# Reordering a Fourier mixing kernel: the last inverse stage later behind its reads, the first transforms sooner, a table in portions, and a bias added from PSUM

## The chip, the cores and the metric

The kernel runs on one core of a Trainium2 chip. The time is device microseconds from start to end of one execution; the span in a profile is some 1.8 us shorter. Each kernel was run several times beside the kernel before on the same chip. A ratio below is the mean time of one kernel's fast runs over that of the other's fast runs of the same rounds, so it is not quite the ratio of the medians quoted beside it.

## The reference

Two layers follow each other on `x` of 8 batches, 3072 positions and 256 channels. Cut to what matters:

```python
X = np.fft.rfft(x, axis=1)                       # along the sequence
Yr = Xr @ w_r - Xi @ w_i + b_r                   # complex product with bias
Yi = Xr @ w_i + Xi @ w_r + b_i
Y  = sign(Y) * maximum(abs(Y) - 0.01, 0)         # soft threshold, each part
y  = np.fft.irfft(Y, n=3072, axis=1)
xk, xr = mixes of y with y shifted by one position
k  = maximum(xk @ w_k, 0)
out = sigmoid(xr @ w_r) * (k * k @ w_v)
```

The transform of length 3072 is split into 96 x 32. So each batch goes through four stages of matmuls ("first", "second" with the mix, "back", "last"), and between first and second, and between back and last, the data goes through DRAM to be turned: A is stored and read back, then V is stored and read back. The "tokens" are the second layer, 6 blocks of 512 positions per batch.

## The kernel before

The program order of every engine is fixed while the kernel is built. A small list scheduler keeps a clock in microseconds and estimates when each buffer will be ready, and emits the unit with the smallest due time among those that its clock holds ready. If the estimate was too early, TensorE stands at that unit, and what is ordered after it waits too (5.5 us for V in the profiled run below). The parts that the change touches:

```python
READ_US, WRITE_US = 7.0, 5.0            # the scheduler's estimates

# first stage: evict, store A, read it back turned
def store(k):
    nc.sync.dma_start(out=Adr[b][:, 8 * q:8 * q + 8, :], in_=a)
    ...                                  # also starts a later batch's load of x
    if q == 3:
        at(k + WRITE_US, fetch)          # fetch: 8 reads of A, 192 KB each, same queue

# mix: z = PSUM; z += bias; y = soft threshold of z
e = copy(k, z, ps, 1.03, 1.22)           # on ScalarE or VectorE
nc.vector.tensor_tensor(out=z, in0=z, in1=bias, op=ALU.add)
nc.vector.tensor_scalar(out=y, in0=z, scalar1=LAM, scalar2=-LAM, op0=ALU.min, op1=ALU.max)
nc.vector.tensor_tensor(out=y, in0=z, in1=y, op=ALU.subtract)

# back: evict V, store it, read it back turned
for q in (2, 3, 0, 1):
    nc.sync.dma_start(out=V2[b, q], in_=Vdr[b][:, 8 * q:8 * q + 8, :])
done["V2", b] = k + READ_US              # when the last stage may be ordered
...
fb += first(b, s - 0.9 * P, s - 0.2 * P) # due times; P = 71.5 us is one batch's period
fa += middle(b, s, s + 0.5 * P)          # second, mix, back
fc += last(b, s + 0.75 * P, s + 0.95 * P)
```

V stores, V reads, A stores, A reads and output stores all leave through one queue, that of SyncE; loads of x leave through GpSimd's.

## Time and profile before

| | before |
|---|---|
| median of whole runs (range), us | 607.5 (602.77 to 610.39), 4 runs; the prediction knew three of them, median 608.08 |
| span of the profiled run, us | 604.4 |
| TensorE busy | 570.7 us, 94% |
| TensorE waits for V from DRAM | 5.5 us |
| time at half clock, without the end | 6.8 us in two stretches |
| start of the last stage, batch to batch | 71.4 us (mean of batches 2 to 6) |

"Busy" is time with an instruction in flight. A group's line ends with the engine's idle time ahead of it and what ended that idle time, as `<-`. "PE" is TensorE, "PEld" its weight loads, "DVE" VectorE, "ACT" ScalarE, and "SPq" the instructions of SyncE that issue DMA. The prediction below shows the lines of before.

### The profile page before, as it was taken

Reading aid. Unit: us, or ns where it says so; the run is one execution under the profiler, and the core shown is the slowest. Engines: PE = TensorE matmul, PEld = TensorE weight load, DVE = VectorE, ACT = ScalarE, POOL = GpSimd, SP = SyncE. Lnnn points to the kernel's source line nnn. Section 1 sums busy time; section 2 is a strip of 40 time slices with the busy share of each in tenths; the row PEclk is TensorE's granted clock in tenths of the full one; section 3 lists DMA queues with packets and bytes.
Section 4 is the critical chain, followed back from the end, with each engine's and each line's share of the span. In section 5 each row is a group of like instructions: output and inputs, shape, how many; then the busy total and the mean of one; then the engine's idle time right before and its main releaser. Section 6 shows DMA issues by size and latency. Waiting matters only on the chain.

```text
span 604.4 us, 12322 instructions
## 1 busy us (share of the span) xinstructions
PE 570.7 (94%) x4823; PEld 430.9 (71%) x4891; DVE 517.6 (86%) x839; ACT 436.3 (72%) x477; POOL 23.9 (4%) x53
## 2 busy tenths in 40 slices
PE   4977999999999999889999999999999999999996
PEld 3856766677767787667776777677776778776775
DVE  7677998789998899958988888979988889989983
ACT  6956986767776777567786768777787777667553
POOL 7001000000000000000000000000000000000000
PEclk9999999999999999989999999999999999999999
DMA  8945849864589555793569935785347834362224
GB/s 149 158 87 129 171 96 240 190 129 106 107 202 213 142 123 119 173 222 99 124 133 225 203 77 117 159 247 125 94 104 186 185 96 89 80 183 50 65 64 102
DMA packets 68878, 84.06 MB, mean 139 GB/s; under 512 B 9042, under 2 KB 53844, under 8 KB 68820
## 3 DMA queue, kind: packets, MB, share of 16 engines
q1 hardware_dynamic: 62916, 68.98, 45.8%
q0 software_dynamic: 5712, 14.03, 14.9%
q8 instruction: 38, 0.62, 0.4%
q10 hardware_dynamic: 192, 0.26, 0.2%
q14 instruction: 20, 0.16, 0.1%
HBM read 50.07 MB, written 47.19 MB: 161 GB/s over the span
## 4 chain that ended last, share of the span: by engine, by line
PE 80%; DMA 7%; DVE 5%; ACT 5%; issue 2%; SPq 1%; POOL 0%; ACTq 0%; POOLq 0%; DVEq 0%
PE banks L655 25%; PE banks L611 24%; PE banks L422 12%; PE banks L638 6%; DMA V<-Vdr 4%; PE banks L448 3%; PE banks L394 3%; PE banks L279 3%; PE banks L525 3%; ACT rl L617 2%; DMA Vdr<-V 2%; DMA xs<-in_x_dram 1%; ACT YT L226 1%; PE banks L352 1%; DVE Y L438 1%
## 5 line engine op out<-in xcount | busy, mean ns | idle before, releaser
L617 ACT ACTIVATE rl<-banks 128x1024 bf16<-128x1024 f32 x192 | 195.5, 1033 | 76.2 <-PE banks L611 75.2
L611 PE MATMUL banks<-xk,wk 128*128 128x512 bf16 x700 | 190.6, 379 | 5.3 <-ACT A L226 0.8
L655 PE MATMUL banks<-wv,k 128*128 128x256 bf16 x1536 | 183.4, 272 | 0.3 <-DVE k L623 0.3
L655 PEld LDWEIGHTS <-k 128*128 128x128 bf16 x1536 | 149.7, 98 | 30.3 <-issue 1.2
L623 DVE TENSOR_TENSOR k<-rl 128x1024 bf16<-128x1024 bf16 x192 | 131.1, 686 | 17.9 <-ACT rl L617 17.2
L611 PEld LDWEIGHTS <-wk 128*128 128x128 bf16 x768 | 73.0, 98 | 59.7 <-issue 3.5
L422 PEld LDWEIGHTS <-XT 128*128 128x128 bf16 x768 | 74.1, 98 | 17.2 <-issue 1.2
L422 PE MATMUL banks<-wr,XT 128*128 128x256 bf16 x384 | 73.3, 272 | 0.5 <-ACT YT L226 0.2
L422 PE MATMUL banks<-wi,XT 128*128 128x256 bf16 x384 | 73.3, 273 | 0.4 <-DVE XT L404 0.4
L589 DVE SCALAR_TENSOR_TENSOR xk<-diff,muk,YT 128x512 bf16<-128x512 bf16 x96 | 70.0, 745 | 0.5
L589 DVE SCALAR_TENSOR_TENSOR xr<-diff,mur,YT 128x512 bf16<-128x512 bf16 x96 | 68.9, 745 | 0.0
L666 DVE TENSOR_TENSOR o<-banks,rg 128x1024 f32<-128x1024 f32 (+1 forms) x49 | 58.7, 1197 | 5.8 <-PE banks L655 5.8
L226 ACT ACTIVATE YT<-banks 128x768 bf16<-128x768 f32 x60 | 46.4, 815 | 21.7 <-PE banks L525 19.0
L226 ACT ACTIVATE XT<-banks 128x1024 bf16<-128x1024 f32 (+2 forms) x46 | 44.9, 982 | 14.5 <-PE banks L394 14.3
L226 ACT ACTIVATE z<-banks 128x1024 bf16<-128x1024 f32 x38 | 38.9, 1024 | 22.0 <-PE banks L422 21.9
L638 PE MATMUL banks<-wrm,xr 128*128 128x256 bf16 x384 | 50.2, 274 | 1.7 <-ACT rl L617 1.5
L226 ACT ACTIVATE A<-banks 96x1024 bf16<-96x1024 f32 (+1 forms) x44 | 44.6, 1015 | 8.8 <-PE banks L279 6.7
L643 ACT ACTIVATE rg<-banks 128x1024 bf16<-128x1024 f32 x48 | 49.5, 1032 | 0.5 <-PE banks L638 0.5
L638 PEld LDWEIGHTS <-xr 128*128 128x128 bf16 x384 | 37.3, 98 | 12.4 <-issue 2.3
L226 ACT ACTIVATE V<-banks 128x1024 bf16<-128x1024 f32 x35 | 36.0, 1029 | 13.8 <-PE banks L448 9.8
L436 DVE TENSOR_TENSOR z<-z,bias 128x1024 bf16<-128x1024 bf16 x48 | 32.9, 686 | 9.5 <-ACT z L226 9.4
L525 PEld LDWEIGHTS <-V 96*128 96x128 bf16 x512 | 27.2, 98 | 13.5 <-DMA V<-Vdr 7.3
(100 smaller groups left out, 448.9 us busy)
## 6 DMA issues: line engine op xcount, KB each, us to landing
out_dram<-o SPq DMA_DIRECT2D x188, 128.0 KB, 2.3
xs<-in_x_dram POOLq DMA_DIRECT2D x32, 384.0 KB, 5.8
Vdr<-V SPq DMA_DIRECT2D x192, 64.0 KB, 1.8
V<-Vdr SPq DMA_DIRECT2D x32, 384.0 KB, 6.6
Adr<-A SPq DMA_DIRECT2D x24, 384.0 KB, 5.3
A<-Adr SPq DMA_DIRECT2D x48, 192.0 KB, 5.6
wk<-in_moe_w_k_dram POOLq DMA_DIRECT2D x1, 512.0 KB, 12.5
wv<-in_moe_w_v_dram POOLq DMA_DIRECT2D x1, 512.0 KB, 13.8
```

What stands on the lines that cost most here:

```text
L226: nc.scalar.activation(out, in_, AF.Copy, bias=0.0, scale=1.0)
L422: nc.tensor.matmul(o, lhs, w[:, c, :], start=(w is wr and c == 0), stop=(w is wi and c == NCD - 1))
L436: nc.vector.tensor_tensor(out=z, in0=z, in1=bias0 if u == 0 else bias, op=ALU.add)
L525: nc.tensor.matmul(pv[:, c, :, i, :], V2[b, n2 // 8][:, n2 % 8, 128 * c:128 * c + 128], FI, start=True, stop=True)
L589: nc.vector.scalar_tensor_tensor(out=m[:, c, :], in0=df[:, c, :], scalar=mu[:, c:c + 1], in1=yp[:, c, :], op0=ALU.mult, op1=ALU.add)
L611: nc.tensor.matmul(ps[:, 512 * f:512 * f + 512], wk[:, c, 128 * ff:128 * ff + 128], xk[:, c, :], start=(c == 0), stop=(c == NCD - 1))
L617: nc.scalar.activation(rl, ps, AF.Relu, bias=0.0, scale=1.0)
L623: nc.vector.tensor_tensor(out=k2, in0=rl, in1=rl, op=ALU.mult)
L638: nc.tensor.matmul(ps[:, 256 * q:256 * q + 256], xr[:, c, 128 * q:128 * q + 128], wrm[:, c, :], start=(c == 0), stop=(c == NCD - 1))
L643: nc.scalar.activation(rg, ps, AF.Sigmoid, bias=0.0, scale=1.0)
L655: nc.tensor.matmul(ps[:, 256 * q:256 * q + 256], K2[t][:, ff, 128 * q:128 * q + 128], wv[:, ff, :], start=(ff == 0), stop=(ff == NCF - 1))
L666: nc.vector.tensor_tensor(out=o[:, lo:hi], in0=ps[:, lo:hi], in1=rg[:, lo:hi], op=ALU.mult)
```

## The change

The intent: order the last stage so late that its read has landed, bring the first transforms forward so that they do not meet that read, let three table evictions go out one by one instead of in a row, and save a pass over z where VectorE evicts it.

```diff
-                    e = copy(k, z, ps, 1.03, 1.22)
+                    a = max(k, free["act"]) + 1.13
+                    if max(k, free["dve"]) + 2.35 <= max(a, free["dve"]) + 1.8:
+                        nc.vector.tensor_tensor(out=z, in0=ps, in1=bs, op=ALU.add)
+                        ...
+                    nc.scalar.activation(z, ps, AF.Copy, bias=0.0, scale=1.0)
+                    ...                       # then the add on VectorE as before
-                    done["V2", b] = k + READ_US
+                    done["V2", b] = k + (READ_US if b == 0 else 11.5)
-                needs = [("y", b, u), "GI"]
+                needs = [("y", b, u), ("GI", u // 2)]
-            fb += first(b, s - 0.9 * P, s - 0.2 * P)
+            fb += first(b, s - 1.2 * P, s - 0.5 * P)
-    tab += [Unit(18.0 + n, 0.5, ["G"], table_gi(n)) for n in range(3)]
+    tab += [Unit(22.0 + 4.0 * n, 0.5, ["G", ("xt", 0, n)], table_gi(n)) for n in range(3)]
```

(The bookkeeping around these lines is cut.) Lines further down shift: L525 of before is L538 after (last stage), L448 is L461 (back), L461 is L474 (V store), L472 is L485 (V read), L611 is L624 and L655 is L668 (tokens).

## The prediction

> **What bounds the kernel now.** I read the engine summary first, then the chain that ended last, the waits of TensorE, and busy time by stretch. The page of the profiled run (span 604.4 us, 606.18 us by the clock that times whole runs):
>
> ```profile
> PE 570.7 (94%) x4823; PEld 430.9 (71%) x4891; DVE 517.6 (86%) x839; ACT 436.3 (72%) x477; POOL 23.9 (4%) x53
> ...
> PE 80%; DMA 7%; DVE 5%; ACT 5%; issue 2%; SPq 1%; POOL 0%; ACTq 0%; POOLq 0%; DVEq 0%
> ```
>
> TensorE is 94% busy and 80% of the chain. The change removes no matmul, so it can only win TensorE's idle time, 604.4 - 570.7 = 33.7 us, and time at a lower clock. Where that lies, by stretch (columns: stretch, length, busy us of PE, PEld, DVE, ACT, POOL, granted clock, DMA share, GB/s):
>
> ```profile
> 0.00:66.00 66.00, 48.69 (x567) 42.11 (x568) 48.96 (x108) 46.96 (x57) 14.27 (x34) 0.97 0.71 136
> 66.00:250.00 184.00, 180.13 (x1447) 133.08 (x1469) 166.90 (x260) 138.90 (x150) 5.56 (x11) 1.00 0.68 152
> 250.00:262.00 12.00, 8.42 (x64) 5.80 (x64) 8.08 (x15) 5.21 (x6) 0.51 (x1) 0.86 0.87 241
> 262.00:545.00 283.00, 278.95 (x2348) 210.66 (x2383) 247.52 (x393) 212.06 (x230) 3.54 (x7) 1.00 0.61 141
> 545.00:605.00 60.00, 54.54 (x406) 39.23 (x411) 46.12 (x66) 33.21 (x36) 0.00 (x0) 0.98 0.29 71
> ```
>
> Idle: 17.3 us in start-up, 3.9 in the long stretch to 250, 3.6 in the 12 us after 250, 4.1 to 545, and a tail that is mostly the last stores. The waits of TensorE name the two causes that the change can touch:
>
> ```profile
> PE banks L525 <- DMA V<-Vdr: 5.5, 6, 2.1
> PE banks L448 <- DVE Y L438: 4.5, 3, 3.1
> ```
>
> L525 is the last inverse stage, waiting for its read-back from DRAM; 1.2 + 0.7 of the 5.5 us are in start-up (batch 0, which the change leaves), 0.3 at 331, and 3.35 at 255, in the timeline of TensorE:
>
> ```profile
> 256.72 0.34 PE L525 MATMUL banks<-FI,V 96*128 96x96 f16 x4 [2.05 <-DMA V<-Vdr]
> 257.94 0.34 PE L525 MATMUL banks<-FI,V 96*128 96x96 f16 x4 [0.87 <-DMA V<-Vdr]
> ...
> 260.56 0.50 PE L525 MATMUL banks<-FI,V 96*128 96x96 f16 x4 [0.43 <-DMA V<-Vdr]
> ```
>
> L448 is the stage before it, waiting for the soft-thresholded Y; all 4.5 us are in batch 0's start-up:
>
> ```profile
> 27.46 0.60 PE L448 MATMUL banks<-Y,GI 128*128 128x256 bf16 x4 [0.46 <-DVE Y L438]
> ...
> 37.26 0.61 PE L448 MATMUL banks<-Y,GI 128*128 128x256 bf16 x4 [0.91 <-DVE Y L438]
> ...
> 43.16 0.94 PE L448 MATMUL banks<-Y,GI 128*128 128x256 bf16 x4 [3.11 <-DVE Y L438]
> ```
>
> **What the Trainium skill says.** "TensorE: Matmul & The Clock Gate", Part 1: an idle window of about 3.4 us halves TensorE's clock, windows run free, and it takes a busy window to restore it. The trace agrees: right after the 3.11 us hole the clock is 0.50 for 43.3 to 46.7, and it is 0.83 in 255 to 260 and 0.82 in 260 to 265. Each such episode lasts 3.4 us and so costs some 1.7 us more. "VectorE: DVE Perf Modes", What auto-detection actually checks: a two-source operation on all-16-bit operands can take two elements a cycle, one with an fp32 operand one. The trace agrees: the 128x1024 bias add on bf16 takes 686 ns, a copy of fp32 from PSUM 1225 ns, and the output's product of an fp32 PSUM operand with bf16 some 1.2 us. "DMA: Bandwidth & Descriptors", Issuing engines are not separate DMA queues: all issuers share 16 DMA engines. The trace agrees as far as it goes: DMA share 1.02 in 255 to 260, where reads of V, loads of x, stores of A and output meet.
>
> **Part 1: bias added from PSUM.** Today each of 48 mixes ends with a copy out of PSUM (10 on VectorE at 1225 ns, 38 on ScalarE at 1024), then add 0.69, clamp 0.43, subtract 0.69 on VectorE. New: if VectorE is free enough, one add straight from PSUM (I take 1.22 us from the copy and the product) replaces copy and add. The rule of the diff prefers it when VectorE's queue is within about 0.6 us of empty, or ScalarE's is long. A unit formerly copied on VectorE saves 0.69; one that moves from ScalarE costs VectorE 1.22 - 0.69 = 0.53 and frees 1.03 on ScalarE. If some 25 of 48 end on VectorE, that is 15 x 0.53 - 10 x 0.69 = +1 us of VectorE and -15 us of ScalarE: nothing for a TensorE-bound stage. What counts is latency in start-up. For the last Y of batch 0, ScalarE began its copy at 39.66 and Y was done at 43.1, 3.4 us, of which 0.55 was VectorE busy with a V copy. Directly: 1.22 + 0.43 + 0.69 = 2.35. So the hole of 3.11 becomes about 2, and those of 0.91 and 0.46 close: 2.4 us. A 2 us hole may or may not empty a clock window; I count 0.6 of its 1.7 us: 1.0. Against that, a little is lost where other start-up work then meets. Net 2.5 us.
>
> **Part 2: table in portions.** Three 1.045 us evictions of the GI table run back to back on ScalarE at 20.9 to 23.7, and XT copies go round them. Spread out, the first Y comes up to 1 us sooner, but TensorE was 4.88 of 5 us busy at 20 to 25. I count 0.5 us.
>
> **Part 3: last inverse stage later.** The order of TensorE is fixed by the kernel's own clock, which takes 7 us for the read. From issue to landing the trace has a median of 6.6 us for one of four reads, and 9 to 11 us for all four. At 255 it failed because the write before the read landed late: issued at 243.28 it took 7.49 us instead of some 1.8, since the x load and an A store shared the engines. Ordering the stage 4.5 us later moves its start from 254.7 to about 259: the reads of the first two quarters (256.7 and 257.9) are in, the last (260.5) almost. Gain there 3.35 + 1.7 of clock, and 0.3 at 331: 5.4 us at most. Does the delay make a hole? In the last batch the stage starts at 536.45, and at 541 there is still some 8 us of token matmuls left before the next batch's tokens, which need about 6.5 us after the stage starts. So it fits, barely.
>
> **Part 4: first transforms 0.3 period (21 us) sooner.** Their A stores and x loads leave the neighbourhood of the V reads. The second transforms can then fill TensorE while the delayed stage waits. But the read of A, at 336 today after the V read at 320, comes to about 315: 1.5 MB taking 10 us, just ahead of the V write and read. That write would then land late in many batches, and eat most of the 4.5 us. Also batch 2's transforms are now overdue when tokens begin: eight evictions of 1.02 us pile up at 66 to 80, where ScalarE has 14.3 of 15 us busy. I set 1.0 us lost for that and 1.7 us of small V waits remaining.
>
> **Sum.** 606.2 - 2.5 - 0.5 - 5.4 + 1.0 + 1.7 = 600.5 us.
>
> **Rivals.** (a) *A new collision*: the A read ahead of the V read delays the latter by 5 us or more in each of five batches, with holes of 2 us and clock drops: +5 to +12, so 606 to 612. For it: A reads take 10 us and share the queue. Against: 4.5 us more allowance. (b) *All holes close*, start-up gains a whole clock episode: 606.2 - 5.4 - 2.4 - 1.7 - 1.5 = 595. For it: TensorE is otherwise full to about 99%. (c) *VectorE becomes the bound*: it is 5.00 of 5 us busy in many stretches; with all 48 on VectorE, 38 x 0.53 - 10 x 0.69 = 13 us more work, part of it exposed: some 605. Against: the rule looks at VectorE's queue. (d) *The 255 hole is chance of that run*: the runs of before span 602.77 to 610.39, so other runs have other holes; a run without it gains only the start-up.
>
> **Range and chances.** 2% faster means below some 596 (from 608.08): needs (b) or a slow base: 0.19. 2% slower needs (a) at its worst: 0.03. Range 594.5 to 606.5.
>
> **What would show it.** Right: TensorE's waits on V from DRAM down from 5.5 to 3 us or less, on Y from 4.5 to about 2; the low clock only at the ends or once; the A read landing before the V read; the direct add near 1.22 us, some 25 times. TensorE busy near 570 still. Wrong: long V waits in several batches, a hole ahead of the last batch's tokens, or more waits at 66 to 85.

## The result

The changed kernel takes **623.93 us** (623.4 to 624.9, 4 runs) against 607.5 us (602.77 to 610.39) of the kernel before: ratio 1.028, interval 1.0212 to 1.0348. It is slower by 2.8%, and outside the predicted range. The profiled run has a span of 621.6 us, 17.2 more than before.

The page of the changed kernel, engine summary and chain of waits:

```profile
PE 581.0 (93%) x4825; PEld 439.2 (71%) x4891; DVE 513.6 (83%) x825; ACT 427.9 (69%) x465; POOL 23.8 (4%) x53
...
PE 83%; DMA 7%; ACT 5%; DVE 2%; issue 1%; POOL 0%; SPq 0%; ACTq 0%; POOLq 0%; DVEq 0%
```

TensorE does the same matmuls, yet is busy 10.3 us longer: part of them ran at half clock. Busy time by stretch (columns as before):

```profile
0.00:66.00 66.00, 51.10 (x564) 45.14 (x565) 47.56 (x104) 44.19 (x54) 13.95 (x34) 0.92 0.73 137
66.00:250.00 184.00, 175.93 (x1397) 130.19 (x1418) 153.71 (x240) 137.35 (x148) 6.20 (x12) 0.98 0.65 152
250.00:262.00 12.00, 11.95 (x85) 8.28 (x85) 11.63 (x18) 7.78 (x9) 0.51 (x1) 1.00 1.11 214
262.00:545.00 283.00, 271.31 (x2239) 204.84 (x2271) 241.02 (x378) 194.60 (x209) 3.15 (x6) 0.98 0.55 133
```

The hole that was in 250 to 262 is gone, but the two long stretches each have holes now: 8.1 us idle where it was 3.9, and 11.7 where it was 4.1. TensorE's waits of the changed kernel:

```profile
PE banks L538 <- DMA V<-Vdr: 13.4, 14, 2.1
...
PE banks L422 <- DVE XT L404: 2.1, 1, 2.1
PE banks L461 <- DVE Y L451: 2.1, 1, 2.1
```

The waits for V went from 5.5 to 13.4 us, in spite of the longer allowance, and they come in each of batches 2 to 6. One of them, in TensorE's timeline of the changed kernel:

```profile
267.78 0.34 PE L538 MATMUL banks<-FI,V 96*128 96x96 f16 x4 [0.53 <-DMA V<-Vdr]
269.06 0.34 PE L538 MATMUL banks<-FI,V 96*128 96x96 f16 x4 [0.93 <-DMA V<-Vdr]
271.21 0.50 PE L538 MATMUL banks<-FI,V 96*128 96x96 f16 x4 [1.81 <-DMA V<-Vdr]
272.30 1.78 PE L538 MATMUL banks<-FI,V 96*128 96x96 f16 x20 [0.59 <-DMA V<-Vdr]
```

The clock follows the holes. The trace shows half clock for 10.2 us from 44.8, 6.8 us from 195.0, 6.8 from 270.1, 3.4 from 348.6 and 3.4 from 420.2: 30.6 us instead of 6.8. At half clock as much as half of that is lost, so up to 12 us more than before. That and the 7.9 us of added V waits make 20 us, against 17.2 in the span; they overlap, since TensorE also waits while the clock is low.

Why V is late stands in SyncE's queue of the changed kernel:

```profile
249.50 1.80 SPq L690 DMA_DIRECT2D out_dram<-o  x4
251.40 4.42 SPq L304 DMA_DIRECT2D A<-Adr  x8
255.92 3.05 SPq L474 DMA_DIRECT2D Vdr<-V  x4
263.48 2.03 SPq L485 DMA_DIRECT2D V<-Vdr  x4
```

In the kernel before, the same queue has the A read last (here batch 4):

```profile
316.80 1.84 SPq L461 DMA_DIRECT2D Vdr<-V  x4
...
320.08 2.79 SPq L472 DMA_DIRECT2D V<-Vdr  x4
...
336.23 3.91 SPq L304 DMA_DIRECT2D A<-Adr  x8
```

In the changed kernel, the last V of the batch had been evicted at 250.4. Its store was issued at 255.9, since the eight reads of A stood in front of it in the queue, for 4.4 us. Then it took until 263.3 to land, and only then could the V read go out. From the trace, the same chain for each batch, in us from eviction of the last V:

| batch | before: store issued, landed | after: store issued, landed | before: last V read landed | after: last V read landed | before: last stage begins | after: last stage begins |
|---|---|---|---|---|---|---|
| 2 | 0.1, 3.3 | 5.1, 12.1 | 14.1 | 21.6 | 12.7 | 16.6 |
| 3 | 0.1, 9.0 | 5.6, 13.0 | 18.8 | 21.9 | 15.0 | 17.4 |
| 4 | 0.7, 3.9 | 4.9, 11.8 | 15.3 | 20.5 | 13.4 | 17.0 |
| 5 | 0.3, 4.1 | 4.5, 11.2 | 14.6 | 19.4 | 13.4 | 17.0 |
| 6 | 0.3, 3.5 | 4.0, 10.8 | 13.7 | 19.9 | 13.4 | 17.3 |

(The last stage begins where its first weight load could start. The profile's views pair only some reads with a landing; the landings here are the last of the 16 counts on the semaphore of each read. They agree with TensorE's own waits: the last one above ends at 272.3, 21.9 us after eviction.) The stage was ordered some 4 us later, as intended, except in batch 3, whose stage had itself waited before. Its data came 5 to 7.5 us later (3 in batch 3, where the store had been late before), in every batch and not just in one.

### The profile page after: what moved, and what is told of

The parts are those of the page before. It is cut to its first block, busy times and chain, and to the rows that moved or that the text cites. A ratio compares the mean times of both kernels' runs of the same rounds, so it can differ in the third digit from the quotient of the medians.

```text
span 621.6 us, 12315 instructions
## 1 busy us (share of the span) xinstructions
PE 581.0 (93%) x4825; PEld 439.2 (71%) x4891; DVE 513.6 (83%) x825; ACT 427.9 (69%) x465; POOL 23.8 (4%) x53
## 4 chain that ended last, share of the span: by engine, by line
PE 83%; DMA 7%; ACT 5%; DVE 2%; issue 1%; POOL 0%; SPq 0%; ACTq 0%; POOLq 0%; DVEq 0%
PE banks L668 27%; PE banks L624 23%; PE banks L422 13%; DMA V<-Vdr 6%; PE banks L651 5%; PE banks L461 3%; PE banks L279 3%; PE banks L394 3%; PE banks L538 3%; ACT rl L630 1%; PE banks L352 1%; DMA xs<-in_x_dram 1%; ACT YT L226 1%; ACT V L226 1%; PE banks L334 1%
## 5 line engine op out<-in xcount | busy, mean ns | idle before, releaser
L624 PE MATMUL banks<-xk,wk 128*128 128x512 bf16 x702 | 189.1, 379 | 4.8 <-DVE xk L602 0.7
L668 PE MATMUL banks<-wv,k 128*128 128x256 bf16 x1536 | 189.0, 278 | 0.7 <-DVE k L636 0.3
L668 PEld LDWEIGHTS <-k 128*128 128x128 bf16 x1536 | 152.1, 100 | 33.5 <-issue 2.1
L624 PEld LDWEIGHTS <-wk 128*128 128x128 bf16 x768 | 74.2, 98 | 57.6 <-issue 2.0
L226 ACT ACTIVATE YT<-banks 128x768 bf16<-128x768 f32 x55 | 42.5, 812 | 35.9 <-PE banks L538 33.3
L226 ACT ACTIVATE V<-banks 128x1024 bf16<-128x1024 f32 x43 | 44.1, 1026 | 22.7 <-PE banks L461 18.9
L226 ACT ACTIVATE A<-banks 96x1024 bf16<-96x1024 f32 (+1 forms) x47 | 47.4, 1030 | 3.9 <-PE banks L352 3.9
L434 DVE TENSOR_TENSOR z<-banks,bias 128x1024 bf16<-128x1024 f32 x26 | 31.8, 1224 | 19.9 <-PE banks L422 19.9
L226 ACT ACTIVATE XT<-banks 128x1024 bf16<-128x1024 f32 (+2 forms) x44 | 43.1, 983 | 6.6 <-PE banks L394 6.0
L538 PE MATMUL banks<-FI,V 96*128 96x96 f16 x512 | 32.6, 218 | 14.0 <-DMA V<-Vdr 13.4
L538 PEld LDWEIGHTS <-V 96*128 96x128 bf16 x512 | 28.4, 105 | 19.5 <-DMA V<-Vdr 15.7
```

Source lines behind the costliest of these rows:

```text
L226: nc.scalar.activation(out, in_, AF.Copy, bias=0.0, scale=1.0)
L434: nc.vector.tensor_tensor(out=z, in0=ps, in1=bs, op=ALU.add)
L538: nc.tensor.matmul(pv[:, c, :, i, :], V2[b, n2 // 8][:, n2 % 8, 128 * c:128 * c + 128], FI, start=True, stop=True)
L624: nc.tensor.matmul(ps[:, 512 * f:512 * f + 512], wk[:, c, 128 * ff:128 * ff + 128], xk[:, c, :], start=(c == 0), stop=(c == NCD - 1))
L668: nc.tensor.matmul(ps[:, 256 * q:256 * q + 256], K2[t][:, ff, 128 * q:128 * q + 128], wv[:, ff, :], start=(ff == 0), stop=(ff == NCF - 1))
```

## The experiments

The theory after the result, **T1**: the earlier first transforms put the read of A in front of the V store and V read, and that is the whole loss. **T2**: the later last stage itself leaves TensorE without work. **T3**: the start-up parts (bias, table) cost it. Four runs take the parts apart.

**no_early**: the changed kernel with the first transforms back at their place.

```diff
-            fb += first(b, s - 1.2 * P, s - 0.5 * P)
+            fb += first(b, s - 0.9 * P, s - 0.2 * P)
```

> The changed kernel with the first transforms back at their old place (0.9 to 0.2 period ahead); bias from PSUM, table portions and the later inverse stage stay. T1 (the earlier transforms put the read of A in front of the V write and V read): the V waits of TensorE fall from 13.4 us to under 4 us, the half-clock episodes between 190 and 430 us vanish, 599 to 605 us. T2 (the later inverse stage itself leaves TensorE without work): still 615 us or more, V waits still over 8 us. T3 (the start-up parts cost it): still over 615 us with the loss ahead of 66 us.

Measured: 603.43 us against 608.14, ratio 0.994 (0.9874 to 1.0005). No wait for V is left in the list of TensorE's waits, and the only half clock ahead of the end is start-up's. SyncE's queue there:

```profile
242.80 1.86 SPq L474 DMA_DIRECT2D Vdr<-V  x4
245.84 0.32 SPq L290 DMA_DIRECT2D Adr<-A  x1
247.73 2.55 SPq L485 DMA_DIRECT2D V<-Vdr  x4
...
261.38 0.84 SPq L304 DMA_DIRECT2D A<-Adr  x2
```

The V store goes out 0.3 us after its eviction (242.5) and the A read comes after the V read.

**early_only**: the kernel before with nothing but the earlier transforms.

```diff
-            fb += first(b, s - 0.9 * P, s - 0.2 * P)
+            fb += first(b, s - 1.2 * P, s - 0.5 * P)
```

> The kernel before with the first transforms 0.3 period sooner and nothing else. T1: the V read is late as in the changed kernel, and the inverse stage is ordered 4.5 us sooner, so V waits of TensorE of 15 to 40 us and 622 to 645 us. T2: about the time before, 604 to 610 us. T3: the same as T2.

Measured: 644.02 us against 608.14, ratio 1.0602 (1.0532 to 1.0673). TensorE's waits:

```profile
PE banks L525 <- DMA V<-Vdr: 27.1, 18, 4.5
```

**late_only**: the kernel before with only the later last stage.

```diff
-                    done["V2", b] = k + READ_US
+                    done["V2", b] = k + (READ_US if b == 0 else 11.5)
```

> The kernel before with the last inverse stage ordered for a read of 11.5 us from batch 1 on, and nothing else. T1: the V wait at 255 us is gone, 600 to 605 us. T2: TensorE runs out of work ahead of the stage or of the next batch's tokens, 615 us or more. T3: as T1.

Measured: 605.27 us against 608.14, ratio 0.997 (0.9914 to 1.0027). V waits are 2.1 us, all of them batch 0's, and the low clock at 258 us is gone. The time is 0.3 us over the expected range and the gain is not clear of noise.

**start_only**: the kernel before with bias from PSUM and table portions (the changed kernel with the two former lines back).

> The kernel before with the bias added from PSUM and the table in portions, and nothing else. T1: 603 to 609 us, a gain of 2 us or a loss of 2 us in the first 66 us depending on the clock there. T2: the same. T3: 615 us or more, with the loss in the first 66 us or with VectorE waits in the steady part.

Measured: 607.22 us against 608.14, ratio 0.9996 (0.9936 to 1.0055): nothing. T1 holds, T2 and T3 fall: neither other part costs anything clear of noise, the earlier transforms alone cost 6.0%, and the later stage hides about half of that.

But moving the transforms moves three transfers: A stores, x loads and the A read. It also changes what TensorE has to do while V is read. **Theory F**: it is the place of the A read. **Rival G**: it is the stores and loads, or the missing work.

**a_read_later**: the changed kernel with only the A read later.

```diff
-                        at(k + WRITE_US, fetch)
+                        at(k + WRITE_US + 16.0, fetch)
```

> The changed kernel with only the read of A put 16 us later in the order, so that it is issued after the V write and V read of the same period; transforms, A stores and x loads stay 0.3 period sooner. Theory F (it is the read of A in front of the V write and V read): last V write lands 2 to 4 us after issue instead of 7, V waits of TensorE under 3 us, 599 to 606 us. Rival G (it is the earlier A stores and x loads, or TensorE has used up the work that filled the V read): V waits stay over 8 us, 617 us or more.

Measured: 602.85 us against 606.92, ratio 0.9939 (0.9892 to 0.9986). SyncE's queue there:

```profile
245.83 2.68 SPq L474 DMA_DIRECT2D Vdr<-V  x4
249.99 1.72 SPq L485 DMA_DIRECT2D V<-Vdr  x4
...
255.75 8.64 SPq L304 DMA_DIRECT2D A<-Adr  x8
```

The V store is issued 0 to 1.1 us after eviction, lands 3.1 to 4.1 us after issue (6.7 to 7.4 in the changed kernel), and one V wait of 0.5 us is left. F holds: with the transforms, A stores and x loads still sooner, moving eight reads takes away the whole 21 us. The edit also moves work, since the scheduler now takes A to be ready 16 us later: the next batch's second stage begins at 272.1, behind the last stage (262.0 to 269.7), where in the changed kernel its first two matmuls went out at 266.9, ahead of it. V's landing is counted from its eviction, so it does not come sooner for that; whether the new order has a share in the 21 us is not taken apart.

**a_read_act**: the changed kernel with the A reads issued from ScalarE's queue, to tell a queue's order (F1) from the sharing of the DMA engines (F2).

```diff
-                            nc.sync.dma_start(out=A2[b, hf][32 * cj:32 * cj + 32],
+                            nc.scalar.dma_start(out=A2[b, hf][32 * cj:32 * cj + 32],
```

> The changed kernel with the reads of A issued from ScalarE's queue at the same place in time, everything else as changed. F1 (V write and V read stand behind the A read in one queue): the last V write lands 2 to 4 us after issue, V waits under 6 us, 602 to 612 us. F2 (not the queue, but the shared 16 DMA engines): the last V write still takes 6 to 8 us, V waits over 9 us, 616 us or more. In both, ScalarE may stall up to 1 us per period at the issue.

Measured: 642.13 us against 606.92, ratio 1.0591 (1.054 to 1.0641). Neither expectation fits the time, since something new came in. ScalarE's timeline:

```profile
187.49 7.82 ACTq L304 DMA_DIRECT2D A<-Adr  x8
195.40 1.94 ACT L630 ACTIVATE rl<-banks 128x1024 bf16<-128x1024 f32 x2 [6.99 <-DMA A<-Adr]
```

ScalarE executes nothing while it gets eight reads out, and TensorE runs out of free PSUM behind it. In sum ScalarE waited 47.9 us at six such places, the longest 10.4 us, where I had expected up to 1 us a period. So the time says nothing of F1 and F2, nor does it help that no V wait is left, since TensorE is late for other reasons. But the stores of V do: in batches 2 to 6 they are issued 0 to 1.1 us after eviction (4.0 to 5.6 in the changed kernel), and still need 6.2 to 7.3 us to land (3.1 to 4.1 in a_read_later). The queue's order is worth about 4 us and the shared engines about 3.3 us of the delay. This agrees with the Trainium skill, "DMA: Bandwidth & Descriptors", Issuing engines are not separate DMA queues; the trace adds what the issue costs a busy compute engine.

**sooner_06**: the changed kernel with the transforms sooner by 0.6 period.

```diff
-            fb += first(b, s - 1.2 * P, s - 0.5 * P)
+            fb += first(b, s - 1.5 * P, s - 0.8 * P)
```

> The changed kernel with the first transforms moved by 0.6 period instead of 0.3 (1.5 to 0.8 periods ahead). F: the A read then comes some 20 us ahead of the last V write and is over by then, V waits under 4 us, 600 to 608 us: twice the move is harmless. G: the more it is moved the worse, 624 us or more.

Measured: 618.23 us against 606.92, ratio 1.0191 (1.0134 to 1.0248). As F says, the A read is over (242.1) ahead of the last V store (254.3), which lands in 3.1 us, and V waits are 1.8 us, all in batch 0. But the time is 10 us over F's range. One new hole is in TensorE's timeline:

```profile
118.80 1.22 DVE L679 TENSOR_TENSOR o<-banks,rg 128x1024 f32<-128x1024 f32 x1 [7.21 <-DMA out_dram<-o]
120.08 0.80 PE L538 MATMUL banks<-FI,V 96*128 96x96 f16 x8 [5.67 <-DVE o L679]
```

In batch 1 the A read went out directly ahead of the V read, output stores stood behind both, VectorE waited 7.2 us for an output buffer and TensorE 5.7 us for VectorE. In the steady part a period takes 71.5 us, where it is 70.2 in no_early (71.4 in the kernel before), with many waits of 0.2 to 0.5 us for evictions; I did not find one cause for those.

**allow_17**: the changed kernel with a still later last stage.

```diff
-                    done["V2", b] = k + (READ_US if b == 0 else 11.5)
+                    done["V2", b] = k + (READ_US if b == 0 else 17.0)
```

> The changed kernel with an allowance of 17 us instead of 11.5 for the V read in the order. F: V waits under 4 us as the stage is ordered behind the late read, and 604 to 613 us, as TensorE may now lack work ahead of the next batch's tokens. G: V waits fall but waits of TensorE for xk or YT of the same size take their place, 617 us or more.

Measured: 611.74 us against 606.92, ratio 1.0092 (1.0033 to 1.015). No V wait is left. An allowance of 17 us is enough for the late V (nothing between 11.5 and 17 was tried), but then little work is left beside the stage: waits for xk (1.8 us) and for VectorE's output product (3.5 us) come up. So allowing for the delay recovers 12 of the 16 us, and the kernel is still slower than before.

**no_table** and **no_bias**: the two start-up parts one at a time, both with the later stage and the transforms at their old place. (no_table takes the table lines of the diff back, no_bias the mix lines.)

> Bias from PSUM and the later inverse stage, without the table portions and without the earlier transforms. If the portions cause the 2.1 us wait of the mix for XT at 37 to 39 us (a GI eviction at 34.0 us stands in front of the XT copy) that wait is gone, the half-clock time in start-up falls from 10.2 to 3.4 us or none, and the time is 2 to 4 us under the run with both (603.4): 599 to 602 us. If bias from PSUM alone causes it (the XT negation stands behind the add on VectorE), the wait stays and the time is 602 to 605 us.

Measured: 602.5 us against 607.75, ratio 0.9924 (0.9892 to 0.9956). The XT wait is 1.7 us (2.1 with portions) and the half clock in start-up still 10.2 us, so the portions did not cause either. The time is just over 602.

> Table portions and the later inverse stage, without the bias from PSUM and without the earlier transforms. If the portions cause the XT wait, it is here too, and Y waits of 4 us in start-up as before as well: 604 to 608 us. If not, 603 to 606 us with no XT wait over 1 us. In both the steady part has no V waits over 1 us, and ScalarE is some 6 us busier than with the bias from PSUM.

Measured: 607.62 us against 607.75, ratio 1.0011 (0.9973 to 1.0048). Y waits rose to 6.1 us. A likely reason is in VectorE's timeline there:

```profile
25.81 0.38 DVE L711 TENSOR_SCALAR GI<-GI 1x128 f16<-1x128 f16 x2 [3.13 <-ACT GI L705]
```

VectorE scales two rows of the table right after its first eviction. With the portions that instruction stands in VectorE's order ahead of an XT copy, waiting 3.1 us for ScalarE, and everything behind it waits as well. Beside late_only (0.997), bias from PSUM gains about 0.5% and the portions lose about 0.4%; the intervals overlap, so both are likely rather than shown.

**early_later**: the kernel before, transforms sooner, A read 16 us later, allowance still 7 us.

```diff
-            fb += first(b, s - 0.9 * P, s - 0.2 * P)
+            fb += first(b, s - 1.2 * P, s - 0.5 * P)
-                        at(k + WRITE_US, fetch)
+                        at(k + WRITE_US + 16.0, fetch)
```

> The kernel before with first transforms 0.3 period sooner (which alone gave 644 us) and the A read put 16 us later, allowance 7 us as before. If the A read is the whole cause of those 36 us, V waits fall from 27 us to under 5 us and the time to 601 to 608 us. If the short allowance or the moved A stores and x loads have a part in it, 612 us or more with V waits over 8 us.

Measured: 606.96 us against 607.75, ratio 0.9991 (0.995 to 1.0033), V waits 3.2 us, all in batches 0 and 1. The A read's place alone makes 644 into 607, without any help of the allowance.

**a_read_8**: the changed kernel, A read 8 us later instead of 16.

> The changed kernel with the A read put 8 us later instead of 16: it should be issued between the V write and the V read, or beside the V read. If what hurts is that the last V write lands late (the V read can't be issued before it), the write lands 2 to 4 us after issue and the time is 602 to 608 us with V waits under 5 us. If the V read beside the A read is what hurts, the V read takes 10 us or more from first issue to last landing, V waits of 8 us or more and 612 us or more.

Measured: 619.45 us against 607.53, ratio 1.02 (1.0157 to 1.0243). Neither expectation holds: in batches 2 to 6 the V store lands in 3.1 to 4.2 us, the V read is complete 8.1 to 8.6 us after its first issue, and TensorE waits for no V (1.5 us in batch 0 remain). It waits for A:

```profile
PE banks L377 <- DMA A<-Adr: 12.7, 3, 4.4
```

The second stage, which the scheduler uses to fill the time of the V read, was ordered for a first half of A after 3.5 us, and the A read, now behind the V read, took 14.6 to 15.9 us in those three periods. The late data had merely changed its name. At 16 us later the scheduler no longer takes it as a filler there: the second stage comes behind the last one.

**Versions to beat both kernels.** best_a is the bias from PSUM, the later stage and the sooner transforms with the late A read, without the portions. best_b is no_table with one line more, which lets batch 1's direct transforms fill TensorE's idle time in start-up; best_c is best_a with that line:

```diff
-            return Unit(..., [("x", b, q), "FT"] + [("mid", 0)] * b, issue)
+            return Unit(..., [("x", b, q), "FT"], issue)
```

> Bias from PSUM, later inverse stage, first transforms sooner with the A read 16 us later, no table portions. From the run with the portions (602.85) minus what the portions cost (about 1 us between 603.4 and 602.5): 600 to 603 us, V waits under 1 us, no small waits for the evictions of A in the steady part.

Measured: 601.96 us against 607.53, ratio 0.9912 (0.987 to 0.9953), as expected.

> Bias from PSUM and later inverse stage, no portions, transforms at their old place, and batch 1's direct transforms no longer held until batch 0's middle stage is ordered. If they fill TensorE's idle 3.7 us between 30 and 42 us and keep the clock up, start-up gains 3 to 8 us: 595 to 600 us. If their evictions delay batch 0's chain on VectorE and ScalarE instead, 602 to 608 us with the first tokens later than 66 us.

Measured: **600.35 us** (600.18 to 600.81) against 607.53, ratio 0.9883 (0.985 to 0.9917). The list of holes in start-up is shorter: no wait for XT, 0.9 us for Y, half clock 3.4 us instead of 10.2; TensorE waits 2.7 us for V of batch 0, where no_table has no such wait. The time is 0.35 us over the range for a gain. Its first 66 us, columns as before:

```profile
0.00:66.00 66.00, 52.19 (x600) 45.12 (x601) 49.80 (x108) 46.60 (x58) 13.97 (x34) 0.97 0.75 141
```

TensorE does 600 matmuls in the first 66 us, where it was 564 in the changed kernel and 567 before.

> Both of the former together: the sum of their differences, 593 to 600 us if the free direct transforms help, 602 to 607 us if they do not.

Measured: 600.48 us against 607.53, ratio 0.9881 (0.9845 to 0.9917). It is the same as best_b, and 0.5 us over its range: with the A read out of the way, the sooner transforms gain nothing. All runs gave correct results.

## Why the prediction was wrong

The step that failed is **part 4**, the earlier first transforms: "That write would then land late in many batches, and eat most of the 4.5 us", and then "1.7 us of small V waits remaining". The mechanism was named, down to the place of the A read ahead of the V store, but two terms of it were mis-sized; 1.7 us of V waits were counted and 13.4 us measured.

- *The delay of V.* I took the store that landed late at 243 us (7.49 instead of 1.8 us) for the model, that is, the shared engines. The store also waited in SyncE's queue, mostly behind the eight A reads, 4.0 to 5.6 us per batch; rival (a) speaks of the shared queue, but part 4 counts nothing for it. From eviction to landing it was 10.8 to 13.0 us instead of 3.3 to 4.1 in the undisturbed batches: some 8 us. A 4.5 us allowance can't hold that, even though the V read itself then ran some 1.5 us faster (8.0 to 9.3 us from first issue to last landing, before 9.6 to 11.3), with A stores and x loads out of its neighbourhood as part 4 said.
- *What a late V costs.* I put rival (a) at +5 to +12 us with a chance of 3% for over 2%. V waits alone came to 13.4 us, and in batches 2 to 5 the group of short waits left a clock window partly idle and low clock followed; with start-up's 10.2 us it was 30.6 us in all instead of 6.8. early_only, where the stage is ordered for a read of 7 us, cost 36 us.

The other steps:

- *Part 3*, the later stage: right. late_only and no_early show no V wait outside batch 0 and no hole ahead of the next tokens (no_bias, with the same stage, has one V wait of 1.0 us at 334). Its size was too large: no_early against start_only is 0.994 against 0.9996, or some 3.4 us, not 5.4, and that is not clear of noise. Perhaps the hole at 255 us is not in each run of the kernel before (rival d): its fastest runs show a mean clock of 0.997, the profiled one 0.993, but only one run has a trace.
- *Part 1*, the bias: 26 of 48 on VectorE at 1224 ns was as predicted (25 at 1.22 us), and the waits for Y fell from 4.5 to 2.1 us. But a wait of 2.1 us for XT took their place, since the negation of XT now stands behind add, clamp and subtract on VectorE, and the half clock in start-up went from 3.4 to 10.2 us. The first batch's last stage ended at 63.0 us, before at 62.7: the 2.5 us were given back.
- *Part 2*, the table: I counted 0.5 us of gain. The runs point to a loss of 1 to 2.5 us (no_early against no_table, no_bias against late_only), within the intervals.
- *Rival (b)* is what the parts give with the bad one taken out and start-up filled: best_b is 600.35 us. *Rival (c)* did not come up; VectorE is 4 us less busy than before.

What stays open: the 1.3 us per period that sooner_06 loses to small waits, and why the kernel before varies by 1.3% from run to run.

## What to carry to other kernels

When work is moved in a fixed order, follow the transfers that it triggers, and ask what each will stand in front of, both in the queue of the engine that issues and in the DMA engines; the compute that moves may be harmless while a read behind it is not. An allowance for a late read only hides a delay that is smaller than the work left to put in front of it, so take the collision away first and tune the allowance after. Short waits that come in groups can cost more than their sum on TensorE: here waits of 0.53, 0.93 and 1.81 us, with 6.8 us at half clock from 270.1 on.

## What the Trainium skill lacked or had wrong

- "DMA: Bandwidth & Descriptors", Issuing engines are not separate DMA queues, says that issuing from several engines only saves the sequencer's issue time, usually small beside the transfer. Here eight reads held SyncE's queue for 4.0 to 4.6 us, beside 10.0 to 11.1 us until the last of them had landed, and the store of V behind them was issued 4.0 to 5.6 us after its eviction, mostly for that reason; from ScalarE the same eight held a computing engine for 7.8 us at one place and cost 47.9 us of its time in all. The section gives no figure for what the issue costs a computing engine.
- "TensorE: Matmul & The Clock Gate", Part 1, speaks of an idle window of 3.4 us, and for another kernel of frequent micro-idles. In the kernel before, the window ahead of the drop at 258.3 was not idle: TensorE was busy 0.71 of its 3.4 us, by a windowed sum. In the changed kernel a window with 1.62 of 3.41 us busy (41.36 to 44.77) was followed by low clock too. The page gives no share at which this happens.
- The same page says that a busy window restores the clock, and gives no share for that either. In the changed kernel's start-up the clock stayed low for three windows (10.2 us) with TensorE busy 3.33, 2.58 and 3.41 of 3.41 us in them, and came back after the third; in the kernel before, one such window with 3.41 us busy was enough. The first of the three held nearly only matmuls of 96 columns; whether their size or the missing 0.08 us is the reason, no run here shows.
